# Seven 256-column second products in six of layer two's pairs, and a new order at the seam of two MoE layers

## The chip, the cores and the metric

The kernel runs on one core of a Trainium2 chip. The metric is the time on the device in microseconds (us) of one execution; lower is better. TensorE (PE) multiplies, PEld is its weight load, VectorE (DVE), ScalarE (ACT) and GpSimd (POOL) work on tiles of 128 partitions, and SyncE (SP) issues the DMAs.

## What is computed

Clustered attention (2 batches, 8 heads, 768 tokens, 64 per head), then two feed-forward layers of 1536 tokens, 512 wide, 2048 hidden. Only the second layer changes here.

```python
def _moe_ref(x, w_in, w_out):
    h = x @ w_in
    g = np.maximum(0.01 * h, h)
    return (g @ w_out).astype(np.float32)

def _moe2_ref(x, w_in, w_out):
    h = x @ w_in
    r = np.maximum(h, 0.0)
    g = r * r
    return (g @ w_out).astype(np.float32)

x = ...
x = _moe_ref(x=x, **moe_kwargs)
return _moe2_ref(x=x, **moe2_kwargs)
```

## The kernel before

**Numbers in two parts.** Each operand of a matmul is held as a rounded high part (`gh`, `wh`, `xh`, `th`) and the rest, a low part (`gl`, `wl`, `xl`, `tl`). A product is three matmuls: high by high, high by low, low by high (`product`, line 914). A high part is one ScalarE pass, a low part one subtraction on VectorE or GpSimd.

**Tiling.** Tokens stand in three blocks of 512 (b = 0, 1, 2), hidden units in 16 blocks of 128, two of which (f, f + 1) are a pair. A layer m (0 or 1; the text says one and two) runs its eight pairs in turn. For each pair the first products give h, the activation gives g, and the second products add g by w_out into `acc` in SBUF, through PSUM banks and a flush on VectorE (`flush`, line 1031). In layer two g is the stationary operand: an output tile is 128 tokens by 512 columns.

**Seven products in place of eight.** For blocks 0 and 1 by the two halves of the contraction, the first products of a pair are seven products P1 to P7 of six matmuls, by Winograd's scheme. Both layers do this (`quad`, line 1061, and `seven`, line 1118) from their fourth or second pair on. The sums of weights are a third block of the pair (j = 2), made by `sum_pieces` (line 232): four GpSimd sums, a ScalarE rounding, a GpSimd low part. P1, P6, P7 and P4 are added up in one PSUM bank U; k1, k6 and k5 are ScalarE copies of a bank between two products (`keep`), and aV, aX, aW are VectorE additions (`add`).

In **layer one** six pairs (`SEVEN`, line 113) do the second products so, too: M1 to M7 by the sums T1 to T4 of the activated tiles B11, B21, B22, B12 and a fourth weight block (j = 3). An M there is two outputs by three matmuls of 512 columns. B11h is the high part of B11, B11f the full value, B11l its low part, and so on; u0, u1 are the tiles of block 2, o0 to o3 its outputs and f0 to f3 their flushes; r1.0 is the flush of the first bank of M1. In **layer two** a pair runs `step_list` (line 1345): the seven first products, then for each of the tiles of blocks 0 and 1 four outputs of three matmuls of 512 columns (`g2`, line 979), 48 in all, and block 2 of the pair before as two fillers between the first products ("behind").

**Order.** All five queues run in the order in which the program is written. In a pair of `seven` that order is a list of words (`SEVEN_QUAD`, line 73, and the lists around it); in `step_list` it is the list of steps, with the preparation of later weights set beside the steps by `TURN`, and at the first pair of layer two by `TURN_SEAM` (line 1393). Weights come as 64-bit words; five pieces make a block of them (`decode_pieces`, line 177): load, magnitude on ScalarE and low word on GpSimd, join on VectorE, high part on ScalarE, low part on GpSimd. In the lists n0.1 is piece 1 of block 0 of the next pair, c3.1 piece 1 of block 3 of this pair (the rounding of the sums), c3.2 its low part. There is one `wraw` buffer and a ring of seven weight buffers.

The lines touched are: `quad`'s `first` and `third` (1069 to 1115), `seven` (from 1118), `step_list` (from 1380) and the two tables of order.

Of the kernel before, what the change touches and what calls it, by code (L numbers as in the profile page):

```python
# [79 lines left out]
    "n1.2 g11 B22h B22f T3 T2 T1h T2h T1l T4 u0 T2l u0h u0f u0l T3h T3l n1.3 n1.4 "  # L80
) + SEVEN_REST + " h4.0 h4.1"
DOTS = {(0, 0): 0, (0, 1): 1, (1, 0): 2}


@with_exitstack
def attention_moe_moe_kernel(
# [25 lines left out]
    RING = 7  # L112
    SEVEN = (4, 6, 8, 10, 12, 14)
    SIDE = 4
# [43 lines left out]
    for m in range(2):  # L158
        for f in range(0, NF, 2):
            blocks += [(m, f, 0), (m, f, 1)]  # L160
            if f >= PLAIN[m] * 2:
                blocks.append((m, f, 2))
            if m == 0 and f in SEVEN:
                blocks.append((m, f, 3))
# [895 lines left out]

    def quad(m, f):
        f0, f1, s = ((m, f, j) for j in range(3))
# [10 lines left out]
        def first():  # L1073
            p(U, lambda k: w_in(f0, k), lambda k: x_in(k, 0), True)
            p1 = tmp()
            nc.scalar.copy(out=p1, in_=U)
            p(V, lambda k: w_in(f0, 2 + k), lambda k: x_in(2 + k, 0), True)
            add(V, V, p1)
            act(m, 0, f, V)

# [8 lines left out]
        def third():  # L1089
            u2, p5 = kept  # L1090
            p(U, lambda k: w_in(s, 4 + k), lambda k: t_in(2, k), False)
            add(X, U, p5)
            x = acts(m, 1, f + 1, X)
            w = acts(m, 1, f, W)
            u = acts(m, 0, f + 1, U)
            if m:
                x.pop(0)()
            p(W, lambda k: w_in(s, 6 + k), lambda k: x_in(2 + k, 1), False)
            if m:
                x.pop(0)()  # L1100
# [12 lines left out]
            w.pop(0)()
            u.pop(0)()

        return first, second, third

    def seven(f, prev, after, later):

        f0, f1, si, so = ((0, f, j) for j in range(4))  # L1120
        k2, ks = range(2), range(HP)
# [43 lines left out]

        def prelu(out, x):
            nc.scalar.activation(out=out, in_=x, func=AF.Prelu, alpha=0.01)

        hi, lo, full = {}, {}, {}

        def high(n, x, active=False):
            hi[n] = gg.tile([128, N], F32R, tag="gh", name="gh")
            lo[n] = gg.tile([128, N], F32R, tag="gl", name="gl")
            if active:
                prelu(hi[n], x)
            else:
                nc.scalar.copy(out=hi[n], in_=x)
# [3 lines left out]

        def active(n, x, sbuf=False):
            full[n] = tmp("t", 3) if sbuf else x
            prelu(full[n], x)

# [15 lines left out]
        def unit(j):  # L1201
            st[f"u{j}"] = bank(1)
            product(
# [12 lines left out]

        def second(out, ws, g, fresh, stop=True):
            wh, wl = ws
            mm = ((wh, hi[g]), (wh, lo[g]), (wl, hi[g]))
            for i, (l, r) in enumerate(mm):  # L1220
                nc.tensor.matmul(  # L1221
# [3 lines left out]

        def w_out(block, c):
            return tuple(w[:, c : c + 128] for w in weights[block])

        def seventh(q, block, c, g, fresh):
# [6 lines left out]
            for j in range(2):  # L1236
                second(st[q, j], w_out(block, c + 128 * j), g, fresh)

        for name, q, block, c, g, b, half in (
# [8 lines left out]
            for j in range(2):  # L1248
                g = f // 2 if f < NF - 2 or name in "2347" else 1
                ops[f"r{name}.{j}"] = lambda q=q, j=j, b=b, g=g, o=2 * half + j: flush(  # L1250
                    0, b, g, o, st[q, j], later=x_low if b == 0 and o > 1 else None
                )

        def last(o):
            ps = st["o", o] = bank((3, 2, 3, 2)[o])
            c = DM + o * 128
            second(ps, w_out(f0, c), "u0", True, False)
            second(ps, w_out(f1, c), "u1", False)

        for o in range(4):  # L1260
            ops[f"o{o}"] = lambda o=o: last(o)
            ops[f"f{o}"] = lambda o=o: flush(0, 2, f // 2, o, st["o", o], later=x_low)
            ops[f"x0.{o}"] = lambda o=o: x_low[0, o](nc.vector)
        for i, q in enumerate(prev):
            ops[f"bh{i}"] = lambda q=q: g2(*q)
        for c, base in (("n", after), ("l", later), ("c", (0, f))):
            for k in range(4):
# [5 lines left out]
        for kk in range(2):  # L1273
            ops[f"h4.{kk}"] = t_by[0][kk]["h4"]
            for name in ("t1", "t2", "t4"):
                ops[f"{name}.{kk}"] = t_by[1][kk][name]
        order = SEVEN_PLAIN if f < 2 * PLAIN[0] else SEVEN_QUAD if f < NF - 2 else SEVEN_LAST
        for name in order.split():
            ops[name]()
# [65 lines left out]
    def step_list(m, f, prev):  # L1345
# [33 lines left out]

        first, second, third = quad(m, f)  # L1380
        seq = [
# [49 lines left out]
    for m in range(2):  # L1431
        turn = 0
        for f in range(0, NF, 2):
# [82 lines left out]
```

## Time and profile before

| | |
|---|---|
| time of three runs | 742.7, 742.91, 742.96 us; median 742.91 |
| the profiled execution | 743.16 us |
| its span, first to last instruction | 741.4 us |
| busy: PE / PEld | 734.1 / 640.3 us |
| busy: DVE / ACT / POOL | 546.3 / 455.0 / 503.6 us |
| layer two | from 485.3 us of the span on |

A line of the timeline gives the start, the duration, the engine, the line of the kernel and the instruction, out<-in; in brackets the idle time before it and what ended it. Matmuls overlap, so their cost is the distance from start to start, not the duration. PEclk is the granted clock of TensorE as a share of 2.4 GHz.

### The profile page before, as it was taken

To read this page: it belongs to the slowest core of one execution; us is meant where nothing else is said; L and a number is where in the kernel's file an instruction comes from. 1 tells how busy PE (TensorE), PEld (TensorE's weight loads), DVE (VectorE), ACT (ScalarE), POOL (GpSimd) and SP (SyncE) were. 2 spreads that over 40 slices of the span, in tenths; PEclk is the share of its full clock that TensorE was granted. 3 is DMA by queue.
4 is the path that set the end of the run, shared out by engine and by line. 5 is a ranking of instruction groups with operands and counts; after the bars stand their busy time and mean duration, and the time that the engine had idled before them with its cause. 6 is when DMAs were issued, how large, how long until landed. Compare 5 with 4: busy or idle time off the path is not lost.

```text
span 741.4 us, 11210 instructions
## 1 busy us (share of the span) xinstructions
PE 734.1 (99%) x4012; PEld 640.3 (86%) x4012; DVE 546.3 (74%) x856; ACT 455.0 (61%) x841; POOL 503.6 (68%) x471
## 2 busy tenths in 40 slices
PE   9999999999999999999999999999999999999998
PEld 8999999999998888888888888887888888888886
DVE  7999999999997535477776866886666666676655
ACT  7988988988998564456365374657634435443430
POOL 6999999999957748676787877899434343343400
PEclk9999999999999999999999999999999999999999
DMA  5684473572603311112121131111212112121004
GB/s 149 165 218 117 107 188 108 111 186 67 172 1 116 113 57 57 57 57 94 59 76 57 57 114 57 57 58 57 100 50 79 57 57 81 45 103 58 1 0 171
DMA packets 16727, 65.52 MB, mean 88 GB/s; under 512 B 3120, under 2 KB 4272, under 8 KB 11680
## 3 DMA queue, kind: packets, MB, share of 16 engines
q1 hardware_dynamic: 16672, 64.81, 29.5%
q8 instruction: 32, 0.52, 0.3%
q14 instruction: 23, 0.19, 0.1%
HBM read 43.02 MB, written 3.15 MB: 62 GB/s over the span
## 4 chain that ended last, share of the span: by engine, by line
PE 89%; POOL 4%; DVE 3%; ACT 2%; issue 2%; DMA 0%; POOLq 0%; ACTq 0%
PE h L919 31%; PE o L997 20%; PE A L583 8%; PE S L486 8%; PE o L1221 7%; PE T L548 7%; PE h L1221 4%; PE S L356 2%; DVE xl L1045 1%; POOL tl L1303 1%; PE warm L296 1%; PE o L1027 1%; ACT e L518 1%; POOL e L535 1%; DVE el L565 1%
## 5 line engine op out<-in xcount | busy, mean ns | idle before, releaser
L173 POOL TENSOR_TENSOR wl<-wt,wh 128x1024 fp32r<-128x1024 f32 x31 | 75.9, 2447 | 60.9 <-ACT wh L172 60.2
L1037 DVE TENSOR_TENSOR acc<-o,acc 128x512 f32<-128x512 f32 x160 | 103.6, 684 | 11.9 <-PE o L997 11.9
L919 PE MATMUL h<-xh,wl 128*128 128x512 f32 x288 | 112.2, 390 | 0.0
L919 PE MATMUL h<-xl,wh 128*128 128x512 f32 x288 | 112.2, 389 | 0.0
L919 PE MATMUL h<-xh,wh 128*128 128x512 f32 x288 | 112.0, 390 | 0.0
L565 DVE TENSOR_TENSOR el<-T,eh 128x512 fp32r<-128x512 f32 x144 | 94.4, 682 | 2.8 <-ACT eh L559 2.0
L535 POOL TENSOR_SCALAR e<-e,r 128x768 f32<-128x768 f32 x96 | 86.2, 908 | 12.7 <-PE T L548 6.8
L508 DVE TENSOR_REDUCE nm<-S 128x1 f32<-128x768 f32 x96 | 90.8, 947 | 3.8 <-PE S L356 2.0
L518 ACT ACTIVATE e<-S,nm 128x768 f32<-128x768 f32 x96 | 87.1, 908 | 10.1 <-DVE ds L384 3.6
L486 PE MATMUL S<-hb 128*128 128x384 f32 (+1 forms) x384 | 89.4, 347 | 0.6 <-DMA hb<-spl 0.5
L559 ACT CAST eh<-T 128x512 fp32r<-128x512 f32 x144 | 79.6, 589 | 8.9 <-PE T L548 8.7
L583 PE MATMUL A<-eh,vv 128*128 128x256 f32 x288 | 80.3, 308 | 0.6 <-DVE xt L605 0.6
L548 PE MATMUL T<-ident,e 128*128 128x128 f32 x576 | 79.7, 273 | 0.5 <-POOL e L535 0.5
L968 DVE TENSOR_TENSOR gl<-h,gh 128x512 fp32r<-128x512 f32 x60 | 40.8, 690 | 43.9 <-ACT h L963 24.5
L583 PE MATMUL A<-el,vv 128*128 128x256 f32 x288 | 72.9, 283 | 0.2 <-DVE el L565 0.2
L997 PE MATMUL o<-wh,gh 128*128 128x512 f32 x184 | 71.7, 390 | 0.7 <-ACT acc L1034 0.7
L548 PEld LDWEIGHTS T<-ident,e 128*128 128x128 f32 x576 | 68.9, 143 | 3.6 <-POOL e L535 0.7
L997 PE MATMUL o<-wh,gl 128*128 128x512 f32 x184 | 71.6, 389 | 0.0
L997 PE MATMUL o<-wl,gh 128*128 128x512 f32 x184 | 71.6, 389 | 0.0
L173 POOL TENSOR_TENSOR wl<-ws,wh 128x1024 fp32r<-128x1024 f32 x18 | 43.3, 2404 | 41.2 <-ACT wh L172 41.2
L953 ACT ACTIVATE t<-h 128x512 f32<-128x512 f32 x48 | 28.0, 599 | 66.4 <-PE h L919 33.6
L919 PEld LDWEIGHTS h<-xh,wh 128*128 128x128 f32 x288 | 54.0, 188 | 11.8 <-DVE gl L1180 0.9
(187 smaller groups left out, 1763.1 us busy)
## 6 DMA issues: line engine op xcount, KB each, us to landing
wraw<-w SPq DMA_DIRECT2D x32, 1024.0 KB, 4.8
hb<-spl SPq DMA_DIRECT2D x14, 576.0 KB, 4.7
hb<-spl SPq DMA_DIRECT2D x42, 192.0 KB, 5.1
rqk<-qk SPq DMA_DIRECT2D x16, 384.0 KB, 3.7
rv<-v SPq DMA_DIRECT2D x8, 384.0 KB, 3.2
out<-q SPq DMA_DIRECT2D x11, 256.0 KB, 2.1
hb<-st SPq DMA_DIRECT2D x56, 24.0 KB, 2.1
hb<-hb SPq DMA_DIRECT2D x5, 144.0 KB, 8.4
```

The costliest lines, as they stand in the source:

```text
L173: return lambda eng=nc.gpsimd: eng.tensor_tensor(out=wl, in0=t, in1=wh.bitcast(F32), op=ALU.subtract)
L486: nc.tensor.matmul(out=s[:, c, 0:HALF], lhsT=hb[0:k, a, i * 128 : (i + 1) * 128], rhs=hb[0:k, b, c * HALF : (c + 1) * HALF], start=(a == 0 ...
L508: nc.vector.tensor_reduce(out=n, in_=s_t[t][:, :, 0:HALF], axis=AX.XY, op=ALU.max, negate=True)
L518: nc.scalar.activation(out=e.rearrange("p (a b) -> p a b", a=2), in_=s_t.pop(t)[:, :, 0:HALF], func=AF.Exp, bias=n_t.pop(t), scale=1.0, ac ...
L535: nc.gpsimd.tensor_scalar(out=e_t[t], in0=e_t[t], scalar1=r_t[t // 2][:, t % 2 : t % 2 + 1], scalar2=1.0, op0=ALU.mult, op1=ALU.mult,)
L548: nc.tensor.transpose(T[:, o : o + 128], e_t[2 * u + b][:, kc * 128 : (kc + 1) * 128], ident)
L565: nc.vector.tensor_tensor(out=el[:, 2 * g : 2 * g + 2, :].rearrange("p a b -> p (a b)"), in0=T_t.pop((u, g)), in1=eh[:, 2 * g : 2 * g + 2, ...
L583: nc.tensor.matmul(out=A, lhsT=w, rhs=m[:, kc, :], start=(kc == 0 and i == 0), stop=(kc == KC - 1 and i == 1),)
L919: nc.tensor.matmul(out=out, lhsT=l, rhs=r, start=(first and i == 0), stop=(i == n - 1), skip_group_check=not first,)
L997: nc.tensor.matmul(out=outs[o], lhsT=l, rhs=r, start=(first and i == 0), stop=(last and i == 2),)
L1037: nc.vector.tensor_tensor(out=a, in0=ps, in1=a, op=ALU.add)
L1221: nc.tensor.matmul(out=out, lhsT=l, rhs=r, start=(fresh and i == 0), stop=(stop and i == 2), skip_group_check=True,)
```

## The change

Layer two's pairs f = 2 to 12 go through `seven`. There the second products become M1 to M7: the sums T1 to T4 are the stationary operand, 128 tokens at a time, and the weights a block of 256 columns, so that an M is 12 matmuls of 256 columns, two half banks at a time. The activation is a ReLU pass and a square pass on ScalarE, where `step_list` has the ReLU on ScalarE and the square on VectorE. The pair f = 2 has an order of its own, `SEVEN_SEAM`, since two products of block 2 of the first pair are left over (bh0, bh1). The last pair stays in `step_list`, now without fillers, and its first tile's activation is written behind two bank copies. At the seam a rounding (2, 1) goes one step back.

```diff
+SEVEN_SEAM = (
+    "c3.0 P1 k1 P2 aV B11h B11f bh0 P6 k6 P5 k5 bh1 B11l n0.1 P7 aX B22h B22f n0.2 P3 aW B12f n1.0 P4 B21h "
+    "B21f c3.1 c3.2 T1 T3 B21l T2 n0.3 n0.4 T1h T2h T1l n1.1 T4 u0 T2l u0h u0f u0l n1.2 T3h T3l n1.3 n1.4 "
+) + SEVEN_REST
...
-    SEVEN = (4, 6, 8, 10, 12, 14)
+    SEVEN = tuple((0, f) for f in range(4, NF, 2)) + tuple((1, f) for f in range(2, NF - 2, 2))
...
-            if m == 0 and f in SEVEN:
+            if (m, f) in SEVEN:
                 blocks.append((m, f, 3))
...
-    def quad(m, f):
+    def quad(m, f, behind=True):
...
-            act(m, 0, f, V)
+            if behind:
+                act(m, 0, f, V)
...
         def third():
             u2, p5 = kept
+            if not behind:
+                act(m, 0, f, V)
...
+        def active_to(out, x):
+            if m:
+                nc.scalar.activation(out=out, in_=x, func=AF.Square)
+            else:
+                nc.scalar.activation(out=out, in_=x, func=AF.Prelu, alpha=0.01)
+
+        def relu(x):
+            if m:
+                nc.scalar.activation(out=x, in_=x, func=AF.Relu)
...
             if active:
-                prelu(hi[n], x)
+                relu(x)
+                active_to(hi[n], x)
...
         def active(n, x, sbuf=False):
+            if n not in hi:
+                relu(x)
             full[n] = tmp("t", 3) if sbuf else x
-            prelu(full[n], x)
+            active_to(full[n], x)
...
-            st[f"u{j}"] = bank(1)
+            st[f"u{j}"] = bank(1 + j * m)
...
+            if m:
+                gh, gl = (x[g][:, o * 128 : (o + 1) * 128] for x in (hi, lo))
+                mm = ((gh, wh), (gh, wl), (gl, wh))
...
             for j in range(2):
-                second(st[q, j], w_out(block, c + 128 * j), g, fresh)
+                if not m:
+                    second(st[q, j], w_out(block, c + 128 * j), g, fresh)
+                    continue
+                for i in range(2):
+                    second(
+                        st[q, j][:, i * K : (i + 1) * K], w_out(block, c, K), g,
+                        fresh and i == 0, o=2 * j + i,
+                    )
+
+        def flushed(b, j, half, ps):
+            a = acc[:, b, 2 * j : 2 * j + 2, half * K : (half + 1) * K]
+            add(a, ps.rearrange("p (a b) -> p a b", a=2), a)
...
-        ((1, 3),), ((1, 4),), ((2, 1),), ((2, 2),),
+        ((1, 3),), ((1, 4),), (), ((2, 1), (2, 2)),
```

Three places show what the change does to the queues. The first is GpSimd at the seam, from the low part of the first-product sums on. Before (numbers tell buffers apart: wraw is a decode step, wl a weight's low part, ws a sum):

```order
L173 TENSOR_TENSOR wl_6094<-ws_6023,wh_6093 128x1024
L1303 TENSOR_TENSOR tl_3777<-q_5909,th_3776 128x512
L205 TENSOR_SCALAR wraw_6028<-wraw_6028 128x1024
L173 TENSOR_TENSOR wl_6199<-wt_6144,wh_6198 128x1024
L205 TENSOR_SCALAR wraw_6180<-wraw_6180 128x1024
```

And with the change, from behind the row tl_3777<-q_5909 on (gl_6141 is the low part of B11, wl_6237 is c3.2, wl_6246 the next pair's first block, gl_6250 and gl_6253 the low parts of T1 and T2):

```order
L257 TENSOR_TENSOR ws_6118<-wt_5851,wt_5978 128x256
L257 TENSOR_TENSOR ws_6118<-ws_6118,wt_5851 128x256
L257 TENSOR_TENSOR ws_6118<-wt_5851 128x256
L257 TENSOR_TENSOR ws_6118<-wt_5978,ws_6118 128x256
L1195 TENSOR_TENSOR gl_6141<-t_6144,gh_6140 128x512
L209 TENSOR_SCALAR wraw_6028<-wraw_6028 128x1024
L177 TENSOR_TENSOR wl_6237<-ws_6118,wh_6236 128x1024
L177 TENSOR_TENSOR wl_6246<-wt_6196,wh_6245 128x1024
L1195 TENSOR_TENSOR gl_6250<-t_6144,gh_6249 128x512
L209 TENSOR_SCALAR wraw_6223<-wraw_6223 128x1024
L1195 TENSOR_TENSOR gl_6253<-t_6243,gh_6252 128x512
```

Four sums, a second weight low part and the low parts of B11, T1 and T2 are new on this queue; two weight low parts stand ahead of T1's and T2's.

The second is ScalarE in the same pair, from the tile W (B12) on, with the change (h_6170 is W, h_6123 is U with B21, wh_6236 is c3.1, gh_6249 and gh_6252 round T1 and T2):

```order
L1181 ACTIVATE h_6170<-h_6170 128x512
L1175 ACTIVATE t_6221<-h_6170 128x512
L1181 ACTIVATE h_6123<-h_6123 128x512
L1175 ACTIVATE gh_6231<-h_6123 128x512
L1175 ACTIVATE h_6123<-h_6123 128x512
L176 CAST wh_6236<-ws_6118 128x1024
L176 CAST wh_6245<-wt_6196 128x1024
L1192 CAST gh_6249<-t_6144 128x512
L1192 CAST gh_6252<-t_6243 128x512
```

Line 1181 is the ReLU, line 1175 the square; the rounding of the fourth weight block stands behind all of B21's passes.

The third is VectorE in the last pair, before (line 1069 adds bank copies, 956 squares, 968 makes a low part; h_7605 is V, h_7607 is X):

```order
L1069 TENSOR_TENSOR h_7605<-h_7605,q_7614 128x512
L956 SCALAR_TENSOR_TENSOR h_7605<-h_7605,t_7625 128x512
L968 TENSOR_TENSOR gl_7624<-h_7605,gh_7623 128x512
L1037 TENSOR_TENSOR acc_3775<-o_7630,acc_3775 128x512
L1037 TENSOR_TENSOR acc_3775<-o_7634,acc_3775 128x512
L1037 TENSOR_TENSOR acc_3775<-o_7638,acc_3775 128x512
L1037 TENSOR_TENSOR acc_3775<-o_7642,acc_3775 128x512
L1069 TENSOR_TENSOR h_7607<-h_7604,q_7660 128x512
```

And with the change:

```order
L1073 TENSOR_TENSOR h_8009<-h_8009,q_8018 128x512
L960 SCALAR_TENSOR_TENSOR h_8009<-h_8009,t_8045 128x512
L972 TENSOR_TENSOR gl_8044<-h_8009,gh_8043 128x512
L1073 TENSOR_TENSOR h_8011<-h_8008,q_8041 128x512
L960 SCALAR_TENSOR_TENSOR h_8011<-h_8011,t_8059 128x512
```

The four flushes of the filler are gone from between the low part of V and the addition into X.

## Rows read from the trace of the kernel before

**Rows 1.** Stretches of layer two and layer one: us, busy us (starts) by engine, PEclk, DMA.
```profile
560.00:590.00 30.00, 30.00 (x134) 24.85 (x133) 19.20 (x28) 13.09 (x19) 12.28 (x9) 1.00 0.20 70
...
408.00:438.00 30.00, 30.00 (x134) 24.73 (x133) 21.35 (x33) 15.76 (x25) 24.09 (x19) 1.00 0.20 70
```

**Rows 2.** Timelines of PE and ACT at the seam: start us, us, engine, line, instruction.
```profile
515.01 0.39 PE L919 MATMUL h<-xh,wl 128*128 128x512 f32 x1
516.08 0.50 PE L997 MATMUL o<-wh,gh 128*128 128x512 f32 x1 [0.68 <-ACT acc L1034]
...
513.98 1.05 ACT L172 CAST wh<-ws 128x1024 fp32r<-128x1024 f32 x1 [1.96 <-POOL ws L253]
```

**Rows 3.** Timeline of PE: two matmuls of 512 columns, 36 starts apart.
```profile
485.32 0.39 PE L919 MATMUL h<-xh,wh 128*128 128x512 f32 x1
...
493.48 0.39 PE L997 MATMUL o<-wh,gh 128*128 128x512 f32 x1
```

**Rows 4.** Timeline of PE: two matmuls of 256 columns, 11 starts apart.
```profile
736.55 0.28 PE L1027 MATMUL o<-wh,gh 128*128 128x256 f32 x1
...
737.86 0.28 PE L1027 MATMUL h<-wh,gl 128*128 128x256 f32 x1
```

**Rows 5.** Groups of instructions, whole run: line engine op, xcount | busy us, mean ns.
```profile
L1037 DVE TENSOR_TENSOR acc<-o,acc 128x512 f32<-128x512 f32 x160 | 103.6, 684 | 11.9 <-PE o L997 11.9
...
L173 POOL TENSOR_TENSOR wl<-ws,wh 128x1024 fp32r<-128x1024 f32 x18 | 43.3, 2404 | 41.2 <-ACT wh L172 41.2
...
L211 DVE SCALAR_TENSOR_TENSOR wt<-wt,wraw 128x1024 int32<-128x1024 int32 x32 | 40.1, 1254 | 13.1 <-POOL wraw L205 7.6 <-ACT wt L198 5.5
L205 POOL TENSOR_SCALAR wraw<-wraw 128x1024 int32<-128x1024 uint32 x32 | 39.2, 1226 | 7.8 <-DMA wraw<-w 5.6
L1180 POOL TENSOR_TENSOR gl<-t,gh 128x512 fp32r<-128x512 f32 x24 | 35.5, 1496 | 11.2 <-ACT gh L1177 9.3 <-ACT t L1167 1.8
L198 ACT ACTIVATE wt<-wraw 128x1024 f32<-128x1024 f32 x31 | 35.3, 1139 | 24.1 <-POOL ws L253 20.8 <-DMA wraw<-w 2.1 <-POOL e L535 1.1
...
L172 ACT CAST wh<-ws 128x1024 fp32r<-128x1024 f32 x18 | 18.9, 1052 | 17.6 <-POOL ws L253 17.6
```

**Rows 6.** Timeline of ACT in layer one's pair f = 10 (P1 starts at 395.42).
```profile
400.18 0.60 ACT L1167 ACTIVATE gh<-h 128x512 fp32r<-128x512 f32 x1
...
401.14 0.61 ACT L1139 COPY q<-h 128x512 f32<-128x512 f32 x1
...
403.20 0.60 ACT L1167 ACTIVATE gh<-h 128x512 fp32r<-128x512 f32 x1 [0.52 <-DVE h L1127]
...
404.51 0.60 ACT L1167 ACTIVATE t<-h 128x512 f32<-128x512 f32 x1 [0.22 <-DVE h L1127]
```

**Rows 7.** Timelines in layer one's pairs f = 8 (to 395.4) and 10.
```profile
387.96 1.05 ACT L172 CAST wh<-ws 128x1024 fp32r<-128x1024 f32 x1 [3.43 <-POOL ws L253]
...
389.52 0.69 DVE L1180 TENSOR_TENSOR gl<-h,gh 128x512 fp32r<-128x512 f32 x1 [0.69 <-ACT gh L1177]
...
391.33 1.28 DVE L1037 TENSOR_TENSOR acc<-o,acc 128x512 f32<-128x512 f32 x2
...
392.69 0.39 PE L1221 MATMUL o<-gh,wh 128*128 128x512 f32 x1
...
402.21 0.39 PE L919 MATMUL h<-xh,wh 128*128 128x512 f32 x1
```

**Rows 8.** Timelines of ACT and DVE in layer two's pair f = 4: X's activation.
```profile
558.02 0.60 ACT L953 ACTIVATE t<-h 128x512 f32<-128x512 f32 x1 [3.34 <-DVE h L1069]
...
560.00 0.69 DVE L968 TENSOR_TENSOR gl<-h,gh 128x512 fp32r<-128x512 f32 x1
```

**Rows 9.** Stretches of PE at the end of the run: us, busy us (starts), PEclk, DMA.
```profile
738.00:739.00 1.00, 0.14 (x2) 1.00 0.70 268
...
740.00:740.50 0.50, 0.00 (x0) 1.00 0.00 0
...
740.80:741.00 0.20, 0.00 (x0) 0.50 0.00 0
```

More of the change, by code (lines that the diff above doesn't have):

```diff
@@ L1116, in quad, with seven @@
         return first, second, third
-    def seven(f, prev, after, later):
-        f0, f1, si, so = ((0, f, j) for j in range(4))
+    def seven(m, f, prev, after, later):
+        f0, f1, si, so = ((m, f, j) for j in range(4))
         k2, ks = range(2), range(HP)
@@ L1164, in seven @@
         ops["aW"] = lambda: add(get("W"), get("W"), st["k6"])
-        def prelu(out, x):
-            nc.scalar.activation(out=out, in_=x, func=AF.Prelu, alpha=0.01)
+        def active_to(out, x):
[6 more added lines that the diff above has]
+                nc.scalar.activation(out=x, in_=x, func=AF.Relu)
         hi, lo, full = {}, {}, {}
@@ L1215, in seven, with second @@
             ops[n + "lD"] = lambda n=n: low(n, nc.vector)
-        def second(out, ws, g, fresh, stop=True):
+        def second(out, ws, g, fresh, stop=True, o=0):
             wh, wl = ws
             mm = ((wh, hi[g]), (wh, lo[g]), (wl, hi[g]))
+            if m:
+                gh, gl = (x[g][:, o * 128 : (o + 1) * 128] for x in (hi, lo))
+                mm = ((gh, wh), (gh, wl), (gl, wh))
             for i, (l, r) in enumerate(mm):
@@ L1224, in second, with w_out @@
                 )
-        def w_out(block, c):
-            return tuple(w[:, c : c + 128] for w in weights[block])
+        def w_out(block, c, n=128):
+            return tuple(w[:, c : c + n] for w in weights[block])
         def seventh(q, block, c, g, fresh):
@@ L1252, in seven @@
                 )
+                if m:
+                    ops[f"r{name}.{j}"] = lambda q=q, j=j, b=b, half=half: flushed(
+                        b, j, half, st[q, j]
+                    )
         def last(o):
             ps = st["o", o] = bank((3, 2, 3, 2)[o])
-            c = DM + o * 128
-            second(ps, w_out(f0, c), "u0", True, False)
-            second(ps, w_out(f1, c), "u1", False)
+            c, n = (DM, DM) if m else (DM + o * 128, 128)
+            second(ps, w_out(f0, c, n), "u0", True, False, o)
+            second(ps, w_out(f1, c, n), "u1", False, True, o)
         for o in range(4):
             ops[f"o{o}"] = lambda o=o: last(o)
-            ops[f"f{o}"] = lambda o=o: flush(0, 2, f // 2, o, st["o", o], later=x_low)
+            ops[f"f{o}"] = lambda o=o: flush(m, 2, f // 2, o, st["o", o], later=x_low)
             ops[f"x0.{o}"] = lambda o=o: x_low[0, o](nc.vector)
@@ L1265, in seven @@
             ops[f"bh{i}"] = lambda q=q: g2(*q)
-        for c, base in (("n", after), ("l", later), ("c", (0, f))):
+        for c, base in (("n", after), ("l", later), ("c", (m, f))):
             for k in range(4):
@@ L1276, in seven @@
                 ops[f"{name}.{kk}"] = t_by[1][kk][name]
-        order = SEVEN_PLAIN if f < 2 * PLAIN[0] else SEVEN_QUAD if f < NF - 2 else SEVEN_LAST
-        for name in order.split():
+        order = {(0, 4): SEVEN_PLAIN, (0, NF - 2): SEVEN_LAST, (1, 2): SEVEN_SEAM}
+        for name in order.get((m, f), SEVEN_QUAD).split():
             ops[name]()
@@ L1378, in step_list @@
             return seq, tail
-        first, second, third = quad(m, f)
+        first, second, third = quad(m, f, bool(behind))
+        behind = behind or [lambda: None] * 2
         seq = [
@@ L1446, in attention_moe_moe_kernel @@
             later = pair_after(*after)
-            if m == 0 and f in SEVEN:
-                seven(f, prev, after, later)
+            if (m, f) in SEVEN:
+                seven(m, f, prev, after, later)
                 prev = []
@@ L1464, in attention_moe_moe_kernel @@
                     piece((*later, k - 3) if k > 2 else (*after, k), j, *eng)
-                if m == 0 and i == 8 and f + 2 == SEVEN[0]:
+                if (m, f + 2) == SEVEN[0] and i == 8:
                     piece((*after, 3), 0)
```

## The prediction

> **What bounds the kernel now.** I read the table of stretches first, then the timelines of the four computing engines side by side, then the table of groups for the price of one instruction. In a 30 us stretch of layer two TensorE is busy throughout and starts 134 matmuls, while VectorE works 19.2, ScalarE 13.1 and GpSimd 12.3 us; the granted clock is 1.00, the 2.4 GHz level [rows 1]. So a microsecond of matmuls taken out of layer two is a microsecond of time, as long as the other three engines, which have room on average, are not late at one place. The one visible loss is at the seam, behind layer two's first pair: the last of 12 first products starts at 515.01 and the next matmul, 0.23 us later by its turn, only at 516.08, because four bank copies on ScalarE were late [rows 2]. That is 0.84 us.
>
> **What is removed.** A pair of layer two spends 48 matmuls of 512 columns on the second products of its two first token blocks; now it spends seven products of 12 matmuls of 256 columns, 84. A 512-column matmul costs 8.16/36 = 0.2267 us from start to start [rows 3]. For 256 columns the kernel has the very same form in its last block of output, 12 of them: 1.31/11 = 0.119 us, with a weight load in front of each [rows 4]. So 10.88 us become 10.00, 0.88 less per pair, and **-5.3 us** for six pairs. This is a poor exchange: an eighth of the columns goes, but 0.119 is more than half of 0.2267. The Trainium skill (TensorE: Matmul & The Clock Gate, Back-to-back issue gap) puts the gap of a warm matmul at columns / 2.4 plus 2.5 ns, which would make the two 216 and 109 ns and the gain about 7.1 us in place of 5.3. Here each matmul costs 10 to 13 ns over its columns, twice per 512 now, so I keep the rows' 5.3.
>
> The two weight additions of the seam also swap places: the high half of the first-product sums was rounded on ScalarE at 513.98, after waiting 1.96 us for GpSimd, and the four bank copies stood behind it [rows 2]. In the new order the copies stand ahead of it. They can start as soon as the banks are done, near 512.5, and end near 514.5, ahead of 515.24. The **0.84 us** go. The rounding then ends at 515.5 and GpSimd's low half at 517.9, where its first reader (P6, at 517.96) asks for it: 0 to 0.2, taken as 0.
>
> **The seam's pair.** This is where I expect the gain to be lost. Count from the start of P7. TensorE: P7, P3, P4 end at 4.1, u0 at 6.8, M1 and M2 at 9.7, u1 at 12.4; then M6 is due, which needs the low half of T2, the low half of its own weights (c3.2), and two flushed banks. ScalarE: four bank copies trail TensorE to 0.7, the decode step takes 1.14 [rows 5] to 1.8; VectorE adds X by 2.3 and joins the next weights (1.25 [rows 5]) to 3.5, and only then adds W, to 4.1. ScalarE then needs two passes for B12 and three for B21 at 0.48 to 0.60 each [rows 6]: 6.7. Behind them comes c3.1, 1.05 [rows 5]: 7.75. Now GpSimd's queue, in its new order: c3.2 2.40, the next pair's low half 2.40, T1's low half 1.50, a decode step 1.23, T2's low half 1.50 [rows 5], 9.0 together: 16.8. VectorE's next join stands ahead of the flush of the first bank and needs that decode step (15.3), so the flush ends at 15.3 + 1.25 + 0.68 = 17.2 [rows 5]. M6 waits from 12.4 to 17.3: **+4.9 us**. Below: ScalarE without any lag (c3.1 ready at 6.8) and GpSimd's quick forms leave 3.3; above, 5.6.
>
> Behind it GpSimd stays behind: T3's low half, the next weights' low half and four sums hold the rounding that T4 stands behind, T4's low half holds two flushes on VectorE, and M4 needs the second. I get M4's bank ready 0.85 us late. If the clock falls in the wait (third rival), slower M6 and M5 fill that same time. **+0.9**, 0 to 2.
>
> **The five other new pairs** run layer one's order, which costs layer one nothing over 0.2 us a pair. What is new is a ReLU pass per tile on ScalarE. Up to T1's rounding there are four, 4 x 0.48 = 1.9 us; ScalarE's idle times there, 0.52 and 0.22, hide 0.7 [rows 6], so T1 is rounded 1.2 us later, or 1.7 if a square waits out its ReLU's full 0.60. GpSimd's low halves start there and run without a gap to the sums; ScalarE's rounding at 387.96 follows them, then T4's, VectorE's at 389.52, and the flush of M7 that begins at 391.33 is done with its first bank at 392.01. M4 asked for it at 392.69 [rows 7]: 0.7 us of slack, and 0.3 more since each product is 12 x 0.119 against 6 x 0.2267. So 0.2 to 0.7 us of wait a pair. One more: P3 started at 402.21 [rows 7] and k5, which it waits for, started at 401.14 and takes 0.6 [rows 6]; one ReLU more makes it 402.23, a wait of 0 to 0.15. I take 0.35 a pair, **+1.75 us**; ends 0 and 4. ScalarE's 13.1 us per 30 become some 19, VectorE's 20 some 23, GpSimd's 12 some 24, as in layer one [rows 1]; none fills.
>
> **The last pair** loses its two fillers, since the pair ahead leaves no third block behind. P1 to P4 now follow each other, and P4 may write its bank only when VectorE's add into X has read it. That add stands behind the low half of B11, which hangs on a chain that the rows have at 1.98 us from ReLU to the start of the low half [rows 8]. The rounding stands behind the bank copies: the second copy starts at 5.63, the ReLU 0.5 later, the low half at 8.1, the add at 8.8 to 9.5. P4 was due at 8.16: **+1.4 us**, 1.0 to 1.8. Without the moved rounding P7 would be the one that waits.
>
> Nothing else moves: loads, DMAs and layer one stand as they were; the flushes' new 2 x 256 form, which the trace does not have, I price as the 0.684 us of the 512 form [rows 5], 0 to 0.1 more, beside other work.
>
> **Sum:** -5.3 - 0.84 + 4.9 + 0.9 + 1.75 + 1.4 = +2.8 us. On the profiled execution's 743.16 us that is 746.0; the runs' median is 742.91, so **745.7 us**.
>
> **Rivals.** About 0.2% (1.5 us) is what a measurement can tell from no change here.
>
> 1. *Faster: GpSimd's chain is not in front of M6.* It decides if c3.1 to T2's low half fit into the 8.3 us between P4's end and M6, to within 1.5 us. Layer one's pairs hide a chain of the same kind, and GpSimd is 60% idle in layer two. Against it: by the rows 9.0 us have to fit behind a ScalarE that is itself 2.6 us behind P4. Price: -6.1 + 1.5 + 0.5 + 1.4 = -2.7, **740.2 us**. Chance 0.24.
> 2. *No change.* Quick forms on GpSimd and no wait in the five pairs: -6.1 + 4.0 + 0.5 + 0.2 + 1.2 = -0.2, **742.7 us**. Chance 0.17.
> 3. *The clock.* At the end of the run TensorE is busy for 0.14 us behind 738.0 and then stops; the granted clock is still 1.00 to 740.5, and 0.50, the 1.2 GHz level, from 740.8 [rows 9]. M6's wait is as long as that. If TensorE comes back at 1.2 GHz, columns take twice their time: M6, M5, M3 are 4.3 us and o0, o1 2.7; half of these at the low level costs 3.5, in place of the 0.9 above: +5.4, **748.3 us**. The Trainium skill (same page, Why this matters for your kernels) warns of idle gaps over about 3 us between bursts of matmuls. By that rule the fall is certain in my forecast's wait; what it costs no row shows, since none has a matmul at 0.50. Chance 0.13.
> 4. *The products don't shrink.* If a 256-column matmul cost what its weight load lasts, 0.188 us, each pair would grow by 4.9 us and the time pass 770. Rows 4 speak against it. Chance 0.02.
>
> **Numbers.** Forecast 0.44, rivals 0.24, 0.17, 0.13, 0.02. Faster is rival 1, 0.24; same rival 2, 0.17; slower the rest, 0.59. The forecast's own range, from the bounds (3.3 to 5.6, 0 to 2, 0 to 4, 1.0 to 1.8), is 742 to 749, not all at one end. The range must reach rival 1's 740.2 and rival 3's 748.3, and leaves out rival 4 and the tails: **740 to 749 us**.
>
> **What would show it.** Right: in the new profile a wait of TensorE at M6 of the seam's pair of 4 to 5 us, with VectorE's flush or GpSimd's low half as its end; GpSimd without a gap for the 9 us ahead of it; 256-column matmuls 0.119 us apart; waits under 0.7 us at M4 in the other pairs; 1.4 us at P4 of the last. Wrong: no wait over 2 us there (rival 1), a granted clock under 1.00 for several us behind it (rival 3), or 256-column starts other than 0.119 apart.

## The result and the profile after

The changed kernel takes 749.26 us, median of five runs (747.99 to 750.6), against 742.91 (742.7 to 743.1): a ratio of 1.0089, 95% interval 1.0078 to 1.0100. It is slower by 6.35 us where +2.8 was forecast, 0.26 us over the end of the range. The profiled execution took 749.53 us with a span of 747.7, 6.3 more than before.

The first view is the page's busy times and its row of the granted clock, which dips in one slice; then the same two stretches as [rows 1] with the changed kernel (columns as there).

```profile
PE 735.3 (98%) x4228; PEld 648.2 (87%) x4228; DVE 557.8 (75%) x874; ACT 486.9 (65%) x901; POOL 571.0 (76%) x525
...
PEclk9999999999999999999999999999989999999999
```
```profile
560.00:590.00 30.00, 29.90 (x170) 25.79 (x170) 20.85 (x32) 18.87 (x30) 22.30 (x18) 1.00 0.16 63
408.00:438.00 30.00, 30.00 (x134) 24.76 (x133) 21.35 (x33) 15.79 (x25) 24.12 (x19) 1.00 0.21 70
```

Layer one's stretch is as it was. Layer two's has 170 matmuls where it had 134, and the three helpers are loaded about as forecast (ScalarE 18.9, VectorE 20.9, GpSimd 22.3 us; forecast 19, 23, 24). No engine is full. The loss is in places, so I cut both executions at the first matmul of a pair's P1 and compare. Of the seam's pair and of the last, 24 matmuls (5.44 us) changed places; they are moved back here.

| part | before | after | change | forecast |
|---|---|---|---|---|
| up to P1 of the seam's pair (f = 2) | 512.52 | 512.40 | -0.12 | 0 |
| the seam's pair | 32.27 | 37.91 | +5.64 | +4.08 |
| five pairs, f = 4 to 12 | 156.40 | 155.63 | -0.77 | -2.65 |
| last pair, to the last matmul | 36.67 | 38.20 | +1.53 | +1.4 |
| sum | | | +6.28 | +2.83 |

Two of the four parts are wrong. In the seam's pair these rows stand around M6; the fences are the timelines of TensorE (the first matmul of u1, the last of u1, M6, o0, M4 and the next pair's P1), GpSimd, VectorE and ScalarE there.

```profile
532.95 0.40 PE L923 MATMUL h<-xh,wh 128*128 128x512 f32 x1
...
535.47 0.39 PE L923 MATMUL h<-xh,wl 128*128 128x512 f32 x1
540.38 0.55 PE L1241 MATMUL o<-wh,gh 128*128 128x256 f32 x1 [4.53 <-DVE acc L1134]
...
545.68 0.60 PE L1241 MATMUL h<-wh,gh 128*128 128x512 f32 x1
...
552.93 0.28 PE L1241 MATMUL o<-wh,gh 128*128 128x256 f32 x1
...
555.75 0.39 PE L923 MATMUL h<-xh,wh 128*128 128x512 f32 x1
```
```profile
531.22 2.42 POOL L177 TENSOR_TENSOR wl<-ws,wh 128x1024 fp32r<-128x1024 f32 x1 [6.28 <-ACT wh L176]
533.58 2.40 POOL L177 TENSOR_TENSOR wl<-wt,wh 128x1024 fp32r<-128x1024 f32 x1
535.94 1.27 POOL L1195 TENSOR_TENSOR gl<-t,gh 128x512 fp32r<-128x512 f32 x1
537.29 1.09 POOL L209 TENSOR_SCALAR wraw<-wraw 128x1024 int32<-128x1024 uint32 x1
```
```profile
538.41 1.22 DVE L215 SCALAR_TENSOR_TENSOR wt<-wt,wraw 128x1024 int32<-128x1024 int32 x1 [1.94 <-POOL wraw L209]
539.56 2.48 DVE L1134 TENSOR_TENSOR acc<-o,acc 128x512 f32<-128x512 f32 x4
```
```profile
547.27 1.05 ACT L176 CAST wh<-ws 128x1024 fp32r<-128x1024 f32 x1 [4.89 <-POOL ws L257]
548.23 0.58 ACT L1192 CAST gh<-h 128x512 fp32r<-128x512 f32 x1
```

The chain is the forecast's, link by link: c3.2, the next pair's low part, T1's low part and the decode step without a gap on GpSimd, then VectorE's join, then the flush, then M6. M6 starts 17.10 us behind P7 (523.28), where 17.3 was forecast. TensorE's gap is 4.91 us, 4.68 over the normal distance. The seam's old wait is gone: the matmul behind the 12 first products starts 2.72 us behind the first of them (512.40 to 515.12), where [rows 2] had a hole.

What the sum lacked follows M6. From 540.38 to 545.68, M6 and M5 take 5.30 us for 24 matmuls that took 2.87 as M1 and M2 just before. The table of stretches says why (us, then busy us and starts of PE, PEld, DVE, ACT, POOL, then the granted clock, the DMA share and GB/s):

```profile
536.00:539.40 3.40, 0.00 (x0) 0.00 (x0) 1.47 (x2) 0.28 (x1) 3.24 (x3) 0.99 0.00 0
539.40:546.10 6.70, 5.71 (x25) 5.66 (x26) 5.29 (x10) 2.62 (x4) 6.62 (x6) 0.50 0.44 157
546.10:549.10 3.00, 3.00 (x20) 2.73 (x19) 2.69 (x5) 1.53 (x2) 1.84 (x3) 1.00 0.00 0
```

The clock fell to 0.50, the 1.2 GHz level, for 6.7 us, from within the wait on. With o0 (1.60 in place of 1.38) that is 2.65 us. The pair then closes: -0.88 - 0.84 + 4.68 + 2.65 = +5.61 of the +5.64.

In the last pair the view of P4 agrees with the forecast (it starts 1.59 us behind the matmul before it, 1.36 over the normal distance):

```profile
719.32 0.39 PE L923 MATMUL h<-xh,wl 128*128 128x512 f32 x1
720.91 0.50 PE L923 MATMUL h<-xh,wh 128*128 128x512 f32 x1 [1.21 <-DVE h L1073]
```

In the five pairs the products did shrink (0.12 us per matmul of 256 columns), but of each pair's 0.88 us only 0.15 is left. Against 0.2267 and 0.119 us a matmul, the pair f = 6 has 0.71 us too much: 0.31 at P3, some 0.2 at M6 and M4, and the other 0.2 spread over the ten switches between 512 and 256 columns and the rounding of the starts. The timelines of TensorE and ScalarE at P3:

```profile
593.54 0.39 PE L923 MATMUL h<-th,wl 128*128 128x512 f32 x1
593.97 0.50 PE L923 MATMUL h<-xh,wh 128*128 128x512 f32 x1
```
```profile
592.85 0.59 ACT L1175 ACTIVATE t<-h 128x512 f32<-128x512 f32 x1
593.33 0.59 ACT L1146 COPY q<-h 128x512 f32<-128x512 f32 x1
```

P3 is due at 593.77 and its bank's copy k5 ends at 593.92, behind the three passes of B11. The first matmul behind it is slow as well.

### The profile page after: what moved, and what is told of

The parts are those of the page before. It is cut to its first block, busy times and chain, and to the rows that moved or that the text cites. A ratio compares the mean times of both kernels' runs of the same rounds, so it can differ in the third digit from the quotient of the medians.

```text
span 747.7 us, 11802 instructions
## 1 busy us (share of the span) xinstructions
PE 735.3 (98%) x4228; PEld 648.2 (87%) x4228; DVE 557.8 (75%) x874; ACT 486.9 (65%) x901; POOL 571.0 (76%) x525
## 4 chain that ended last, share of the span: by engine, by line
PE 93%; DVE 2%; ACT 2%; POOL 1%; issue 1%; POOLq 0%; ACTq 0%; DVEq 0%
PE h L923 32%; PE o L1241 16%; PE h L1241 9%; PE A L587 8%; PE o L1001 8%; PE S L490 8%; PE T L552 7%; PE S L360 2%; ACT e L522 1%; PE warm L300 1%; DVE nm L512 1%; PE o L1031 1%; DVE el L569 1%; ACT eh L563 0%; POOL wl L177 0%
## 5 line engine op out<-in xcount | busy, mean ns | idle before, releaser
L177 POOL TENSOR_TENSOR wl<-ws,wh 128x1024 fp32r<-128x1024 f32 x24 | 57.7, 2402 | 50.2 <-ACT wh L176 50.2
L1195 POOL TENSOR_TENSOR gl<-t,gh 128x512 fp32r<-128x512 f32 x48 | 71.8, 1513 | 28.2 <-ACT gh L1192 21.3
L202 ACT ACTIVATE wt<-wraw 128x1024 f32<-128x1024 f32 (+1 forms) x33 | 36.7, 1113 | 46.1 <-POOL ws L257 42.6
L1134 DVE TENSOR_TENSOR h<-h,q 128x512 f32<-128x512 f32 x33 | 23.1, 699 | 55.8 <-PE h L923 46.7
L923 PEld LDWEIGHTS h<-xh,wl 128*128 128x128 f32 x288 | 54.1, 188 | 11.4
L490 PEld LDWEIGHTS S<-hb 128*128 128x128 f32 (+1 forms) x384 | 62.3, 190 | 1.7 <-ACT e L522 1.1
L923 PEld LDWEIGHTS h<-xl,wh 128*128 128x128 f32 x288 | 54.2, 188 | 10.6
```

The source lines that it names most:

```text
L177: return lambda eng=nc.gpsimd: eng.tensor_tensor(out=wl, in0=t, in1=wh.bitcast(F32), op=ALU.subtract)
L490: nc.tensor.matmul(out=s[:, c, 0:HALF], lhsT=hb[0:k, a, i * 128 : (i + 1) * 128], rhs=hb[0:k, b, c * HALF : (c + 1) * HALF], start=(a == 0 ...
L923: nc.tensor.matmul(out=out, lhsT=l, rhs=r, start=(first and i == 0), stop=(i == n - 1), skip_group_check=not first,)
L1195: eng.tensor_tensor(out=lo[n], in0=full[n], in1=hi[n].bitcast(F32), op=ALU.subtract)
```

## The experiments

All edit the changed kernel. The kernel before ran beside each group, with medians of 742.74, 743.31, 742.79, 742.95 and 742.74 us. For the seam one more number is read from each trace: from the first matmul of u1 to P1 of the next pair. It is 22.80 us in the changed kernel and would be 15.3 without any wait (36 matmuls at 0.2267, 60 at 0.119). In most runs the time is 1.8 to 1.9 us over the span; in about a third of the changed kernels' runs it is 2.0 to 4.1 over, and in none of the 79 of the kernel before. I have no cause for it, so the parts of the traces count for more than medians half a microsecond apart.

### First group: one suspect each

**Fill the wait.** One product of u1 is computed twice, for nothing.

```diff
-            product(st[f"u{j}"], ...)
+            for _ in range(2 if (m, f, j) == (1, 2, 1) else 1):
+                product(st[f"u{j}"], ...)
```

> The product u1 of the seam's pair is computed twice (12 matmuls of 512 columns more, 2.7 us, the same result), so TensorE works through more than half of its wait at M6; nothing else moves. Theory (the clock falls in the wait and its price adds to the wait): M6 starts when it did, 540.4, the granted clock stays 1.00, M6 and M5 take 2.9 us in place of 5.3, and the bank that M4 needs is then the next thing late, by about 1.2 us; 1 to 1.5 us less than the changed kernel, about 748. Rival A (the clock is the whole of it, nothing is late behind it): 2.6 us less, about 746.7. Rival B (the forecast's reading: slower M6 and M5 only fill a wait that is there anyway): no change, 749.3.

748.25 us (747.58 to 748.49), ratio 1.0074 [1.0062, 1.0087]. Adding 2.7 us of work made the kernel about 1 us faster, as the theory had it, but not in its way. TensorE stood still in front of M6 for 1.85 in place of 4.53 us, and yet the clock did not stay at 1.00: it was 0.50 for 3.2 us, M6 and M5 take 4.53 us, and u1 to P1 is 22.02. So the clock's price shrinks with the gap, and rival A's and rival B's times are both off. One of the five runs kept a granted clock of 1.00, and its span of 746.6 us is no shorter than the 745.7 to 746.5 of the others: as far as one run tells, the low clock filled time here that M4 would have waited. The row is from its table of stretches (columns as above):

```profile
541.80:545.00 3.20, 3.20 (x16) 3.18 (x15) 2.56 (x5) 0.32 (x1) 3.12 (x3) 0.50 0.51 212
```

**Shorten GpSimd's chain**: n0.3 and n0.4 behind u0l.

```diff
-T2 n0.3 n0.4 T1h T2h T1l n1.1 T4 u0 T2l u0h u0f u0l n1.2
+T2 T1h T2h T1l n1.1 T4 u0 T2l u0h u0f u0l n0.3 n0.4 n1.2
```

> In the seam's pair the next pair's first weight block is rounded and its low half made behind the low half of T2 (and u0's) in place of ahead of T1's; GpSimd's queue in front of T2's low half is 2.4 us shorter. Theory (M6's wait is GpSimd's queue): M6 starts 2.2 to 2.6 us earlier, the wait is 2.0 to 2.5 us, the clock stays at 1.00 or nearly: 3.5 to 5 us less than the changed kernel, 744.3 to 745.8. Rival (M6 waits for its own weights, c3.2, or for banks that are flushed late for another reason): the wait stays over 4 us, 749.

748.76 us (748.16 to 750.25), 1.0090 [1.0076, 1.0103], 3 us over the theory's end. M6's wait fell by one low part, 4.53 to 2.25, so GpSimd's chain does set it. But the clock fell all the same (M6 and M5 take 4.67 us), and more than half of the gain came back as a wait of M4, which the change did not show; u1 to P1 is 21.52. TensorE's timeline:

```profile
537.77 0.36 PE L1241 MATMUL o<-wh,gh 128*128 128x256 f32 x1 [2.25 <-DVE acc L1134]
...
551.24 0.35 PE L1241 MATMUL o<-wh,gh 128*128 128x256 f32 x1 [1.62 <-DVE acc L1134]
```

**k5 ahead of B11f** in the pairs f = 4 to 12.

```diff
+            steps = steps.replace("B11h B11f P5 k5", "B11h P5 k5 B11f")
```

> In layer two's pairs f = 4 to 12 ScalarE makes the full value of B11 behind the copy k5 in place of ahead of it, so that k5 is done 0.5 us earlier. Both theories expect P3's wait of about 0.35 us a pair to go. Theory 1 (the waits of a pair lie on one chain: T4's rounding behind GpSimd's sums sets when M4 can start, counted from ScalarE's passes, not from P3): M4's wait grows by what P3's loses, time unchanged within 0.5 us, 749. Theory 2 (P3's wait is a loss of its own): 5 x 0.35 = 1.7 us less, 747.5.

748.84 us (746.83 to 750.3), 1.0082 [1.0069, 1.0096]. The median cannot tell the theories apart; the trace can. P3's wait is gone in every pair, and four of the five pairs last 30.75 in place of 31.1 us (617.84 to 648.59, for one). In the first, M6 now waits 0.38, and the pair is 0.17 us longer. Over the five it is 1.23 us of the 1.7 that the second theory had.

**Split the last pair's activation**: V's ReLU and square ahead of P7, its roundings behind the addition into X.

```diff
-            if not behind:
-                act(m, 0, f, V)
+            v = [] if behind else acts(m, 0, f, V)
+            for g in v[:2]:
+                g()
...
             add(X, U, p5)
+            for g in v[2:]:
+                g()
```

> In the last pair the rounding and the low half of B11 are written behind the addition into X, so that VectorE adds as soon as P7 is done. Theory (P4 waits because the addition stands behind B11's low half): P4's wait of 1.36 us goes to 0 to 0.2, 1.2 to 1.4 us less than the changed kernel, about 748. Rival (P4 would then wait for something else, or the first tile's low half comes too late for its products): no gain, 749.3.

747.85 us (747.02 to 749.12), 1.0074 [1.0061, 1.0086], 1.4 less than the change, as the theory had it. P4's wait is gone, and its 42 first products take 9.61 us where they took 11.03 (the first matmul behind them starts at 719.95, P1 at 710.34).

### Second group: the seam's two waits

**c3.1 and c3.2 ahead of P7**, where their sums are ready (e5); **n0.3 and n0.4 late as well** (e6); **T4 ahead of n2.1 and n2.2** in all six pairs (e7); and **with k5 and the last pair** (e8). The cuts show the lists of words that result.

```diff
-B11l n0.1 P7 aX ... P4 B21h B21f c3.1 c3.2 T1
+B11l n0.1 c3.1 c3.2 P7 aX ... P4 B21h B21f T1
...
-r6.1 n2.1 n2.2 o0 f0 M3 r3.0 T4h T4l r3.1
+r6.1 o0 f0 M3 r3.0 T4h T4l n2.1 n2.2 r3.1
```

> Only the rounding of the seam pair's fourth weight block and its low part (c3.1, c3.2) go ahead of P7; its sums are done at 522.4 us, the low part ran at 531.22 to 533.64. Theory: GpSimd's row of work in front of VectorE's join sets when M6 starts, so M6's wait falls from 4.5 us by one low part, to 2.2, as in the run with n0.4 moved; the clock falls for about 3 us instead of 6.8, which gives back 0.6 more; and here all of GpSimd's row is early, so M4's wait of that run (1.6) does not come: next P1 2.5 to 3.0 us earlier than after the change, span about 744.5, median 746.5. Rival: M4's wait comes whenever M6 is early, since GpSimd's later sums end when they end: then the gain is 1.3 as in that run, median 748.

746.15 us (745.22 to 747.59), 1.0039 [1.0026, 1.0052]: 3.1 us less for moving two words, as the theory had it. M6 waits 2.39, M4 does not, u1 to P1 is 19.82.

> e5's edit and n0.3, n0.4 behind u0l as well. Theory of the wait: M6 finds its flush done, wait below 0.4 us; and since TensorE does not stand still, the granted clock stays 1.00 and M6 with M5 take 2.9 us instead of 5.3. Then the third wait: M4 stands behind T4's low part, behind a rounding (n2.1) that waits for GpSimd's sums, so M4 waits 2 to 3 us. Next P1 about 4 us earlier than after the change, median about 745. Rival, the clock falls for the new shape of the matmuls and not for the wait: M6 and M5 still take 4.6 to 5.3 us with no wait before them; median 747 to 748.

748.0 us (746.86 to 749.36), 1.0067 [1.0055, 1.0079]. The theory of the wait missed: M6 still waits 1.72 us. The time is the rival's, but its reason is not. VectorE's rows show the next link, u0's low part and the join in front of the flush, with GpSimd no longer late:

```profile
535.26 0.69 DVE L1195 TENSOR_TENSOR gl<-h,gh 128x512 fp32r<-128x512 f32 x1 [2.60 <-ACT h L1175]
535.87 1.22 DVE L215 SCALAR_TENSOR_TENSOR wt<-wt,wraw 128x1024 int32<-128x1024 int32 x1
537.00 2.48 DVE L1134 TENSOR_TENSOR acc<-o,acc 128x512 f32<-128x512 f32 x4
```

The clock did stay at 1.00 through M6 and M5 (behind a gap of 2.10 us; the two take 2.94), so the shape of the matmuls is not what makes it fall. The row is from its table of stretches:

```profile
538.00:547.50 9.50, 9.50 (x65) 8.81 (x65) 6.29 (x12) 3.28 (x6) 8.26 (x8) 1.00 0.32 110
```

M4 then waits 2.14 us, as expected, and behind that gap of 2.52 us the clock falls; u1 to P1 is 21.22.

> e6's edit, and in layer two T4's high and low part stand ahead of the rounding n2.1 and its low part n2.2 in every one of the six pairs. Theory: M4's wait at the seam goes (below 0.4 us), and in the five other pairs the 0.1 to 0.25 us that M4 waits: next P1 at about 549 us, 7 us earlier than after the change, last matmul about 7.5 us earlier; median 741.5 to 742.5. Rival: the weights of the next pair, rounded later, become late: the next pair's P6 waits, and the median stays at 744 to 745.

746.2 us (744.24 to 746.79), 1.0034 [1.0022, 1.0046]. The mechanism is there: M4 does not wait, the clock is 1.00, u1 to P1 is 17.44, 5.4 us less than in the change. The median is 4 us above the forecast: M6's wait of 1.74 is still in it, three of the five runs have 2.8 to 3.6 us beyond the span, and two have a granted clock of 0.997. A stretch of the profiled run also settles whether the DMA traffic beside M6 and M5 (157 GB/s in the change's slow stretch) is what slows them: here they run at 1.00 and take 2.95 us with 306 GB/s beside them (columns as above).

```profile
538.00:541.00 3.00, 2.99 (x25) 3.00 (x26) 3.00 (x6) 2.44 (x5) 3.00 (x3) 1.00 0.87 306
```

> e7's edit, with k5 ahead of B11f in layer two's six pairs of seven products and with the last pair's activation split around its add (both as run before). Theory: the three waits are separate, so the gains add up: 0.35 us in each of five pairs less a wait of M6 once, and 1.4 us in the last pair, 2.8 us below e7: median 738.5 to 740, below the kernel before (742.7). Rival: what k5 frees is taken by M6 and M4 in each pair as in the one pair of that run: then 1.4 us below e7, 740.5.

741.18 us (740.39 to 744.99, 12 runs), 0.9983 [0.9971, 0.9994]: 0.2% faster than the kernel before, and 1.2 us above the theory's end; that M6's wait (1.7 in e6 and e7) makes the difference is not shown. Its runs spread over 4.6 us: the eight with a granted clock of 1.00 take 740.39 to 741.37, the four below it 742.99 to 744.99. The profiled one is the longest (0.995): a load of weights landed late, ScalarE's magnitude for it stood in front of u0's activation, M6 waited 3.26 us and the clock fell. ScalarE's timeline:

```profile
533.45 1.14 ACT L202 ACTIVATE wt<-wraw 128x1024 f32<-128x1024 f32 x1 [1.45 <-DMA wraw<-w]
```

### Third group: what is left in front of M6

**The join n1.2 and its followers behind u1l** (e9, on e8), and **n1.1 behind u0l** (e10, on e9).

```diff
-T1l n1.1 T4 u0 T2l u0h u0f u0l n0.3 n0.4 n1.2 T3h T3l n1.3 n1.4 M1 M2 ... u1l n2.0
+T1l T4 u0 T2l u0h u0f u0l n1.1 n0.3 n0.4 T3h T3l M1 M2 ... u1l n1.2 n1.3 n1.4 n2.0
```

> e8's edit, and at the seam n1.2, n1.3 and n1.4 (join, rounding, low part) stand behind u1l. M6 waits for the flush r1.0, and in e6 VectorE ran u0's low part (to 535.9 us), then the join (535.87 to 537.0), then r1.0. Theory: the join in front of the flush is what is left of M6's wait that can be moved; the flush starts 1.1 us earlier, M6's wait falls from 1.7 to 0.6 us, median 741.2 - 1.1 = 740.1. Rival: M6 waits for T2's low part from GpSimd or for the bank itself, and the wait stays at 1.7, median 741.2.

742.73 us (741.98 to 743.86), 0.9999 [0.9990, 1.0008]. M6's wait fell to 0.61, as expected, and the time rose: M3 waits 1.1 behind the join that is now late, and the next pair's P6 waits 1.4 for k1.

> e9's edit, and n1.1 (magnitude on ScalarE, low word on GpSimd, both of which wait for the load of the words) behind u0l. In the profiled run of e8 that load landed 1.0 us later, ScalarE's magnitude stood in front of u0's activation, and M6 waited 3.3 us where it waited 1.7 in e6. Theory: with n1.1 behind, no step ahead of M6 hangs on a load; M6's wait is below 0.3 us, the granted clock is 1.00 through the seam in every run, and the span no longer spreads by 4 us from run to run but by under 1; median 739.0 to 739.6. Rival: the magnitude and the join come late now and M4 or the next pair's P6 waits for a weight instead; median 740 to 741.

742.4 us (741.67 to 743.27), 0.9995 [0.9986, 1.0004]. No wait at M6, and the spread is down to 1.6 us, though four of the eleven runs have a granted clock of 0.997 or 0.998. But the rival was right in kind, and its price was too low: M3 waits 1.9 and P6 1.3. Moved waits cost as much as the one removed.

### Fourth group: the join in its place, and the seam alone

**The join between the flushes of M1 and M2, n1.3 and n1.4 behind u1f** (e11, otherwise e10), and **this list at the seam alone** (e12: the five pairs' roundings, k5 and the last pair as the change has them).

```diff
-r1.0 r1.1 r2.0 r2.1 B22l l0.0 u1 u1h u1f u1l n1.2 n1.3 n1.4 n2.0
+r1.0 r1.1 n1.2 r2.0 r2.1 B22l l0.0 u1 u1h u1f n1.3 n1.4 u1l n2.0
```

> As e10, but the join n1.2 stands between the flushes of M1 and those of M2, and n1.3, n1.4 behind u1f instead of behind u1l. In e10 M6 had no wait, but the join came 2 us later on VectorE, the flushes r6 and r5 behind it, and M3 waited 2.3 us; the sums on GpSimd ended at 553.1 us and k1 of the next pair came late, 1.5 us. Theory: the join is due between those two: M6 without wait, M5 waits about 0.5 us for r2.0, M3 and k1 in time; 2.8 to 3.3 us below e10, median 739.2 to 739.8, with a spread of under 2 us. Rival: ScalarE's rounding n1.3 now delays u1's high part or the sums stay late: M3 or o0 waits 1 to 2 us, median 740.5 to 741.5.

741.27 us (740.6 to 741.82, 12 runs), 0.9970 [0.9954, 0.9985]. M6 does not wait, M5 0.36, M3 not; u1 to P1 is 16.24, and all twelve runs lie within 1.2 us. It is 1.5 us above the forecast, since k1 of the next pair is late in spite of it (P6 waits 1.3 us). The time is the rival's, the place is not: neither M3 nor o0 waits.

> The change with e11's list at the seam alone: the roundings of the five other pairs, k5 and the last pair as the change has them. It tells what the seam's order alone costs. Theory: M6's wait and the low clock together were 7 us of the change's time, of which M4's wait, behind the rounding n2.1, takes back 1.5: median 743.5 to 744.5. Rival: M4's wait takes back 3 us and a second fall of the clock with it, as in e6: median 746 to 747.

748.75 us (746.72 to 751.62), 1.0068 [1.0049, 1.0088]. The theory fell, and the rival was too small. With M6 on time, M4 waits 3.48 us and the clock falls behind it: u1 to P1 is 21.50. Three of the eleven runs kept a granted clock of 1.00, with spans of 744.4 to 744.7 us; the other eight have 745.7 to 747.8. ScalarE's rounding n2.1 waits for GpSimd's sums until 545.88, and T4's rounding stands behind it; the first row is TensorE's, the next two are ScalarE's, and the last is from the table of stretches.

```profile
550.08 0.35 PE L1241 MATMUL o<-wh,gh 128*128 128x256 f32 x1 [3.48 <-DVE acc L1134]
```
```profile
545.88 1.05 ACT L176 CAST wh<-ws 128x1024 fp32r<-128x1024 f32 x1 [6.74 <-POOL ws L257]
546.83 0.58 ACT L1192 CAST gh<-h 128x512 fp32r<-128x512 f32 x1
```
```profile
551.00:554.60 3.60, 3.60 (x14) 3.02 (x13) 1.44 (x3) 1.17 (x1) 2.49 (x3) 0.53 0.02 5
```

### Fifth group: T4 alone, and the next wait

**T4 ahead of n2.1 and nothing else** (e13); **e11 with n0.1 behind k1 in the pair f = 4** (e14).

```diff
+            if f == 4:
+                steps = steps.replace("n0.1 P1 k1 P2", "P1 k1 n0.1 P2")
```

> The change with only T4's high and low part ahead of the rounding n2.1 and its low part n2.2 (the order of e7), the seam's list as the change has it. Theory: at the seam M4's wait hides behind M6's, so the move gives nothing there; in the five other pairs M4 and M6 lose the 0.1 to 0.25 us that they wait: about 0.6 us in all, median 748.3 to 748.9. Rival: the rounding was what delayed the seam as a whole, and the move alone gives the 5 us by which e12 and e11 differ at the seam: median 744 to 745.

749.02 us (748.78 to 749.23), 1.0084 [1.0070, 1.0098]; u1 to P1 is 22.83, as in the change. In the five other pairs it gives 0.63 us, as its theory had it. Alone the move gives nothing at the seam; together with M6's it gives 5.3 us there (e12 against e11). There are two waits on two chains that end near each other, and either covers the other.

> e11 with n0.1 (a magnitude on ScalarE that waits until GpSimd's sums have freed its buffer) behind k1 in the pair f = 4. In e11 k1 stood behind it and P6 waited 1.3 us. Theory: P6 starts 1.4 us earlier, and what is late next is aV and P5 by nothing: median 739.8 to 740.2. Rival: the pair waits for its weight sums (c3) or for n0 later, at M1 or P4, and the time stays at 741.2.

740.22 us (739.68 to 741.24), 0.9968 [0.9957, 0.9980]: the best version, 2.5 us below the kernel before. P6 is on time; the wait moved on to P3, which waits 1.1 us for k5, and the pair f = 4 is 0.96 us shorter than in e11. Its later pairs last 30.6 us, 0.18 over the bare sum of their matmuls; the stretch that had 170 matmuls has 173:

```profile
560.00:590.00 30.00, 30.00 (x173) 26.50 (x172) 21.57 (x32) 18.44 (x30) 23.34 (x19) 1.00 0.19 71
```

## Why the prediction was wrong

**The direction and the place were right.** The second products shrank as priced (24 matmuls take 2.87 us, 2.86 by the rows), the seam's old wait went, M6 waits 4.68 us (forecast 4.9) on the chain that was written out, and P4 of the last pair waits 1.36 us (forecast 1.4). e2, e5 and e4 move those waits by what the steps in them cost. By the gap that the Trainium skill (TensorE: Matmul & The Clock Gate, Back-to-back issue gap) gives for a warm matmul, the estimate for the products was 7.1 us in place of 5.3; the 0.12 us of the new matmuls bears out the rows' 5.3. The "10 to 13 ns" over the columns are 12 to 13 by the rows' own numbers.

**The first step that failed is "Behind it ... +0.9, 0 to 2".** It held that a fallen clock would only fill time that M4 waited anyhow. Measured are 2.65 us of low clock, and M4 does not wait at all. The estimate of M4's lateness was not far off, though: its bank is free about 4.2 us after n2.1's rounding starts (545.88 to 550.08 in e12, 547.05 to 551.24 in e2), so by that distance, an inference, M4 could have started near 551.5 in the changed kernel, 1.2 us behind its turn at the full clock (552.93 less 2.65). It starts at 552.93, behind M6's wait and the low clock. The two parts overlap, as the text said, but the longer one was the clock's, and the sum took the shorter. That was the third rival, rated 0.13 though the forecast's own wait of 4.9 us brought it on: [rows 9] have the clock at 0.50 less than 3 us behind the last matmul. Its price there, 3.5 us, was a third over what the rows now show.

**The second is "+0.35 a pair".** It measures 0.73, inside its bounds of 0 to 4 us for the five, but the 0.35 lay near the low end of the text's own 0.2 to 0.85. P3 was taken as 0 to 0.15 and costs 0.31, because k5 ends 0.15 us late and the matmul behind the wait starts slowly. M6 and M4 cost 0.2, the low end of what was written. The rest, some 0.2 in ten changes of form, was not in the sum; it is what e14 still shows in its later pairs, where no wait is left (0.18). e3 shows P3's part by taking it away, e13 0.08 a pair at M4.

With 2.65 for 0.9 and 5 x 0.73 for 1.75 the forecast's sum is +6.5, against +6.28 measured.

**What the runs add.** The loss of the seam is not one wait that can be taken out. Two chains hold M4: the one through M6 (GpSimd's low parts, VectorE's join, then the low clock) lets it start at 552.93, the one through T4 (GpSimd's sums, then the rounding in front of T4) near 551.5 by the inference above. Removing either leaves the other: 1.3 us gained by e12, nothing by e13. With both moved it is 6.6 (e11, 22.80 to 16.24; its other edits lie behind that stretch).

## What to carry to other kernels

A forecast wait of several microseconds on TensorE needs two more lines in its sum: the work at the low clock behind it, and the wait that stands next when it is removed. When an edit takes a wait away and the time stays, measure a fixed distance (here u1 to the next P1) in both traces and look for the wait that has taken its place; combine edits before giving up on each. Where two queues hand work to each other, an instruction that waits for a slow one (a rounding behind GpSimd's sums, a magnitude behind a load) should stand behind everything that is already due, but no later than its own reader allows: in e9 and e10 the moved join made M3 and P6 wait for longer than M6 had.

## What was unexpected in the hardware

The granted clock in the seam's pair over all traces: behind gaps between two matmul starts of 1.45 (e9), 2.01 (e2), 2.10 (e6), 2.12 (e7) and 2.30 us (e10) it stayed at 1.00; behind 2.24 (e1), 2.52 (e6), 2.63 (e2) and 2.78 (e5) it fell to 0.50 for some 3 us, behind 3.87 (e12) for 3.4, and behind 3.65 (e8) and 4.91 (the change) for 6 to 7, each time with matmuls running again for most of it. In e1 it fell only at 541.6, 1.5 us after M6 had started. The rule that the prediction took from the Trainium skill (TensorE: Matmul & The Clock Gate, Why this matters for your kernels) speaks of gaps over about 3 us; here the fall is seen from 2.24 on, and 2.30 went without, so the gap alone does not decide it. At 0.50 a matmul of 256 columns starts every 0.21 us and one of 512 every 0.43, against 0.119 and 0.227. A switch between the two forms costs some 0.02 us, an estimate from the 0.18 us in ten switches of e14.
